# Preparing two units of a decayed linear attention with one scan, in a new written-out order

## The chip, the cores and the metric

The program runs on one core of a Trainium2 chip. The metric is the device time of one execution in microseconds (us). Three runs of the kernel before took 474.7, 475.89 and 476.5 us; the median is 475.89.

## What is computed

Three stages follow each other, in 32-bit arithmetic. The first is a linear attention with a state that decays by channel, for 4 batches, 8 heads, 768 tokens and 48 channels a head:

```
cur   = outer(u * k[t], v[t])
y[t]  = r[t] @ (state + cur)
state = w[t][:, None] * state + outer(k[t], v[t])
```

Its output, 768 x 384 per batch, is the x of a gated block: `h = gelu(x @ w_in)`, its first half u, its second half v normalised over 512 channels; `v_s = w_sg @ v_n + b_sg` mixes the tokens; the result is `x + (u * v_s) @ w_out`. Of that, a third block makes a causal convolution with 5 taps, its sigmoid as a gate, and `(gate * (x @ w_val)) @ w_out2`.

## The kernel before, in words

**Units.** The attention is cut into units: a batch, one of 3 segments of 256 tokens, one of 4 pairs of heads. There are 48, numbered 0 to 47, twelve to a batch. A pair of heads lies on 128 partitions (two times 64, of which 48 carry channels and 16 zeros). Within a unit the tokens are cut into 4 chunks of 64.

**Preparing a unit** (letters are the words of the written-out order). `F` (function `suffix`) is a scan on VectorE over 260 columns that multiplies decays from the right, and a reciprocal of 4 columns; `E` (`prefix`) is a scan from the left which starts each chunk from that reciprocal, in tile D1E. `L` multiplies r by E on GpSimd, `K` multiplies k by F (on GpSimd in batch 0, on VectorE later), and `q` is r times k on VectorE in batches 0 and 1. The input of a unit, decays, k and r, comes in one DMA of 386.5 KB (`pk`); later batches keep two buffers for it.

**Visiting a unit.** TensorE turns k into rows (`t`), makes the 64 x 64 scores of the chunks (`s`), the k-v products (`B`, in `kv`) and the tokens' outputs (`C`). A 32-bit product shows as two matmul records. All of a visit's results share PSUM tile p: k-v products, outputs, transposes and scores have columns of their own in it. The units of odd number in batch 0 use two banks c1 and c2 in its place. Between products ScalarE evicts (`kx`, `gx`, `ox`, `yc`), VectorE masks the scores (`mx`), steps the state (`a`, `z`) and adds outputs (`yx`).

**The dense blocks.** `hv`, `u`, `vs`, `wo`, `val` and `out` are products with 384 or 512 moving columns, three passes each for precision. Words like `vs0` stand for three of them. `ln` normalises a 128 x 512 piece of v: three operations of ScalarE, one of VectorE (`rs`, from the sum of squares), a power on GpSimd, one more of ScalarE and one of VectorE. Weights arrive as 64-bit numbers and are decoded on ScalarE and VectorE (`dec`).

**The order.** The kernel's code writes all instructions into a log under their words; then the string `SCHEDULE` names the words one by one, and each engine gets its instructions in that order. Each engine runs its own list in order and waits at the head of it. Batch 0's attention and the weights' decoding run before the dense products of batch 0; from then on a batch's dense products are interleaved with the visits of the next batch. The last batch has dense products alone. Ahead of the first products, and within and between the visits of batch 0, stand bf16 products on constants, of no use to the result (`wps`, `wm`); three of 256 columns make one word.

The change touches `PARTS` (buffers), `suffix` to `ruk` and `kv` in `unit`, `shared`, `run_loads`, `attention`, `hv`, `out_step`, `first_loads`, and the whole of `SCHEDULE`.

Of the kernel before, what the change touches and what calls it, by code (L numbers as in the profile page):

```python
# [25 lines left out]
C = 64  # L26
# [29 lines left out]
ini0 pk0 zp0 wps0 pk1 pk2 ld0 wl0 ld1 wl1 nat0 F0 wl2 E0 sv0 q0 L0 F1 wl4 K0 pk3 E1 s0 dec0 sv3 wm4  # L56
F2 L1 wl3 wm4 wm0 dec0 t0 K1 q1 nat1 kx0 dec1 t1 dec0 kx1 s1 E2 sv9 B0 dec1 wm1 gx1 L2 mx1 gx2 wm2
mx0 dec1 wm9 dec2 K2 sv10 wm9 dec1 wm10 pk4 gx0 ox0 kx2 B1 dec0 dec4 sv1 wm10 dec2 wm3 a0 dec2 t2 a0
C0 sv2 dec2 sg0 s2 dec1 wm5 ox1 yc0 kx3 wm6 ow2 dec4 gx4 wm7 F3 ow0 sg1 wm8 kx4 gx5 wm11 ow6 K3 z0
wm12 mx2 dec3 wm13 dec0 pk5 gx3 wm15 wl5 ow3 dec4 ox2 pk7 ow7 q2 B2 ow1 dec2 spl1 sv4 wm14 a1 spl0  # L60
dec3 wm15 wm16 a1 dec3 wm16 E3 q3 L3 mx3 yx0 yx1 wm21 dec4 t3 dec3 s3 C1 dec4 wm17 gx7 dec3 wm18
spl10 wm19 F4 yc1 wm20 wl6 ox3 ow5 yd0 wm23 ow9 sv6 spl9 wm21 spl10 K4 wm22 pk6 wm22 spl2 z1 wl7 mx4
E4 yc2 wl8 ow4 U4 sv5 kx5 spl9 L4 gx6 sv7 B3 yx2 pk10 dec5 a2 wm24 sv8 gx8 q4 ow10 s4 sg2 a2 ow8 C2
dec5 F5 pk11 t4 ox5 K5 ox4 mx5 yc3 ow11 z2 ow13 dec5 pk8 wm27 kx6 ow14 E5 wm27 wm28 kx7 U5 wm28 dec5
gx11 pk9 L5 t5 spl3 yx3 gx10 mx6 ow15 dec5 gx9 yd1 wm29 yx4 spl11 a3 s5 q5 ow12 a3 C3 F6 yc4 dec6
nat2 yd2 B4 spl11 K6 wm25 yc5 wm29 yx5 wm30 dec7 mx7 wm30 E6 yd3 ox6 xT0 ow17 wm26 z3 xTo0 spl0 L6
gx12 gx13 xTo0 hv0 kx8 ow19 a4 gx14 spl1 hv0 spl2 t6 dec7 xT1 dec6 a4 s6 dec6 xTo1 B5 dec7 spl5 a4
C4 dec7 spl5 xTo1 hv1 ox7 kx9 U6 mx10 ow18 F7 hv0 spl3 ow20 sg5 gx17 ox8 gx15 ow23 z4 mx8 yc6 kx10
a5 ow16 wm31 K7 ow22 mx9 wm31 yx6 gx16 wm32 q6 ln0 wm32 a5 hv1 dec6 a5 wm33 E7 hv1 F8 spl4 L7 wm33
wm34 ln1 t7 q7 C5 E8 B6 s7 dec7 L8 wm34 gx18 z5 gx20 a6 ow21 K8 kx11 yx7 ln1 gx19 q8 yc7 U7 t8 yd4  # L70
yc8 a6 ox9 s8 spl4 ow26 mx11 B7 spl8 yx8 a6 C6 ow25 sg4 F9 gx23 K9 gx21 z6 U9 wm35 a7 gx22 yd5 ow24
wm35 mx12 wm36 U8 a7 wm36 E9 ow27 ox10 t9 ox11 kx13 kx12 q9 L9 ow31 B8 yx10 ow30 ln0 yx9 ow29 a7 ln0
yc10 s9 F10 ow28 C7 spl8 nat3 sv11 kx14 yc9 ln0 sg3 yx11 xT2 E10 pk12 wm37 ln1 xTo2 wm37 wl9 wm38
gx26 xTo2 hv2 ox12 gx25 K10 gx24 mx13 ln1 z7 a8 wm38 yd6 a8 hv2 ow34 q10 yc11 ow35 a8 yd7 ow33 hv2
F11 U10 L10 ow32 C8 ln2 mx14 B9 ln0 s10 pk13 E11 xT3 t10 q11 wm39 L11 ox14 gx27 wm39 wm40 yc12 gx28
a9 wm40 kx15 K11 yc13 xTo3 yx12 mx15 a9 gx29 s11 q12 kx16 ox13 a9 C9 ow38 ln2 F12 U11 ln2 B10 spl7
K12 ow37 t11 spl7 ow36 wm41 yx13 kx17 xTo3 hv3 gx30 gx32 a10 gx31 yd8 spl6 wm41 wm42 a10 q13 ox15
wm42 ow39 spl6 ow43 mx16 B11 yx14 ln2 mx17 a10 C10 ow40 E12 ow42 yc14 hv3 gx34 F13 L12 ow41 gx33
ox17 hv3 gx35 yx16 ox16 yc15 a11 ow47 yd9 pk14 yx15 yc16 ln1 ow45 s12 ln3 t12 K13 a11 dec6 a11 C11
E13 kx18 wm43 ow44 ln2 L13 ow46 wm43 spl12 nat4 yx17 xT4 mx19 sv12 yc17 F14 yd10 kx19 t13 xTo4 pk15  # L80
s13 spl13 B12 spl12 yd11 ln3 xT5 mx18 dec8 ln3 xTo4 hv4 kx20 spl13 gx36 xTo5 hv4 dec8 ln3 E14 hv4
# [118 lines left out]
def tile_kernel(ctx, tc, pk, sv_, rk_, v_, u_, misc_, w_in, w_sgT, b_sg, w_o1, w_val,  # L200
# [843 lines left out]
```

## Time and profile before

| | |
|---|---|
| median of 3 runs | 475.89 us |
| profiled execution | 474.3 us, span 472.5 us |
| TensorE matmul busy | 450.6 us, 95% of the span |
| weight loads busy | 406.3 us, 86% |
| VectorE busy | 385.0 us, 81% |
| ScalarE busy | 266.9 us, 56% |
| GpSimd busy | 162.3 us, 34% |
| bytes moved | 48.91 MB, mean 103 GB/s |

Times in the profile are us from the start of the span. A busy TensorE is not one at its peak, since the records of pipelined products overlap. PEclk is the share of the full clock that was granted. All instructions carry line 969, the place where the log is played; they are told apart by tile names (vps is `vs`, ups is `u`, c is `wo`, o is `out`, kh and L are `K` and `L`).

### The profile page before, as it was taken

What the parts mean: (1) busy time and instruction counts of PE and PEld (TensorE: products, weight loads), DVE (VectorE), ACT (ScalarE), POOL (GpSimd) and SP (SyncE); (2) the same over time, 40 slices, a digit from 0 to 9 for tenths busy, and PEclk for the clock granted to TensorE, in tenths of its full rate; (3) what the DMA queues carried; (4) which work ended last, traced back from release to release, by engine and by line L of the source; (5) the groups of instructions that cost most, each with busy time, mean ns of one, the idle gap of its engine ahead of it and who ended that gap; (6) DMA issues with size and microseconds to landing.
All of it is one profiled execution on the core that took longest, in us unless ns stands there. A gap on an engine that the chain in (4) does not pass through costs nothing.

```text
span 472.5 us, 13805 instructions
## 1 busy us (share of the span) xinstructions
PE 450.6 (95%) x5556; PEld 406.3 (86%) x5556; DVE 385.0 (81%) x944; ACT 266.9 (56%) x786; POOL 162.3 (34%) x221
## 2 busy tenths in 40 slices
PE   6879899989999999999999999999999999999996
PEld 3666677878979988999999979999999889999995
DVE  5999789999999878978999889847998785337693
ACT  2577789744844469642645388642634696224253
POOL 3245565341622466245132635342213313000200
PEclk9999799999999999999999999999999999999999
DMA  8974053543414452124324522134114000100002
GB/s 278 354 261 167 1 163 111 187 154 114 130 50 116 157 185 68 60 74 152 125 67 135 171 92 85 51 85 135 54 39 147 10 2 1 50 2 0 1 1 100
DMA packets 27088, 48.91 MB, mean 103 GB/s; under 512 B 3088, under 2 KB 17168, under 8 KB 27024
## 3 DMA queue, kind: packets, MB, share of 16 engines
q1 hardware_dynamic: 27024, 48.03, 31.7%
q8 instruction: 43, 0.70, 0.6%
q14 instruction: 21, 0.17, 0.1%
HBM read 43.30 MB, written 4.72 MB: 102 GB/s over the span
## 4 chain that ended last, share of the span: by engine, by line
PE 77%; DVE 9%; ACT 5%; issue 1%; DMA 1%; SPq 0%; ACTq 0%; DVEq 0%
PE vps L969 19%; PE p L969 13%; PE hv L969 10%; PE c L969 9%; PE ups L969 9%; PE o L969 8%; PE val L969 7%; PE a L969 2%; DVE cvp L969 1%; DVE st L969 1%; ACT st L969 1%; ACT vg L969 1%; DVE y L969 1%; DVE F L969 1%; DVE vps L969 1%
## 5 line engine op out<-in xcount | busy, mean ns | idle before, releaser
L969 PE MATMUL vps<-wsg,vnt 128*128 128x384 f32 x576 | 115.5, 339 | 1.4 <-DVE gt L969 0.7
L969 PEld LDWEIGHTS vps<-wsg,vnt 128*128 128x128 f32 x576 | 100.3, 188 | 3.0 <-ACT ut L969 1.6
L969 PE MATMUL ups<-x,win 128*128 128x384 f32 x288 | 61.4, 340 | 0.8 <-DVE gl L969 0.8
L969 ACT ACTIVATE st<-p,F 128x48 f32<-128x48 f32 x144 | 40.3, 304 | 38.0 <-PE p L969 36.7
L969 POOL TENSOR_TENSOR L<-pk,E 128x256 f32<-128x256 f32 x38 | 28.3, 744 | 94.7 <-PE p L969 32.9
L969 PE MATMUL c<-gl,late 128*128 128x384 f32 x288 | 59.9, 339 | 0.0
L969 PE MATMUL hv<-win,x 128*128 128x512 f32 x216 | 59.3, 405 | 0.3 <-ACT x L969 0.3
L969 DVE SCALAR_TENSOR_TENSOR cvp<-x,cw_col,cvp 128x384 f32<-128x384 f32 x84 | 50.6, 613 | 2.1 <-ACT cvp L969 1.6
L969 PEld LDWEIGHTS ups<-x,win 128*128 128x128 f32 x288 | 50.6, 188 | 1.7 <-DVE gl L969 1.1
L969 PEld LDWEIGHTS c<-gl,late 128*128 128x128 f32 x288 | 50.2, 188 | 1.0
L969 DVE SCALAR_TENSOR_TENSOR st<-st,F 128x48 f32<-128x48 f32 x128 | 39.3, 307 | 14.0 <-ACT st L969 13.0
L969 PE MATMUL o<-late,ml 128*128 128x384 f32 x216 | 46.9, 343 | 0.2
L969 PEld LDWEIGHTS hv<-win,x 128*128 128x128 f32 x216 | 38.7, 188 | 8.3 <-DVE x L969 0.9
L969 PE MATMUL val<-x2hl,late 128*128 128x384 f32 x216 | 43.6, 340 | 0.8 <-ACT ut L969 0.8
L969 POOL TENSOR_TENSOR x<-x 128x384 f32<-128x384 f32 x24 | 25.4, 1070 | 44.7 <-DVE cvp L969 43.0
L969 PEld LDWEIGHTS o<-late,ml 128*128 128x128 f32 x216 | 37.9, 188 | 2.8 <-DVE ml L969 1.4
L969 PEld LDWEIGHTS val<-x2hl,late 128*128 128x128 f32 x216 | 37.5, 188 | 1.9 <-ACT ut L969 1.1
L969 ACT ACTIVATE gl<-vps 128x384 fp32r<-128x384 f32 x29 | 14.3, 493 | 33.8 <-DVE vps L969 20.1
L969 POOL TENSOR_TENSOR y<-s,y 128x96 f32<-128x96 f32 x48 | 22.2, 469 | 32.2 <-DVE y L969 17.1
L969 DVE TENSOR_TENSOR_SCAN F<-pk,D1F 128x260 f32<-128x260 f32 x40 | 28.9, 722 | 4.5 <-DMA pk<-in_pk_dram 4.3
L969 POOL TENSOR_TENSOR rstd<-rstd,misc 128x1 f32<-128x1 f32 x24 | 15.6, 650 | 46.0 <-DVE rstd L969 32.3
L969 ACT ACTIVATE ut<-ups 128x384 f32<-128x384 f32 x32 | 15.7, 490 | 25.5 <-PE ups L969 20.6
(133 smaller groups left out, 944.5 us busy)
## 6 DMA issues: line engine op xcount, KB each, us to landing
pk<-in_pk_dram SPq DMA_DIRECT2D x40, 386.5 KB, 3.5
v<-in_v_dram SPq DMA_DIRECT2D x12, 384.0 KB, 4.9
out_dram<-ot SPq DMA_DIRECT2D x24, 192.0 KB, 1.9
rk<-in_rk_dram SPq DMA_DIRECT2D x12, 384.0 KB, 3.3
sv<-in_sv_dram SPq DMA_DIRECT2D x39, 96.0 KB, 3.0
bits<-in_w_in_dram SPq DMA_DIRECT2D x6, 512.0 KB, 7.4
room_l<-in_pk_dram SPq DMA_DIRECT2D x7, 386.5 KB, 6.7
bits<-in_w_o_dram SPq DMA_DIRECT2D x7, 384.0 KB, 4.2
```

The costliest lines, as they stand in the source:

```text
L969: f(*a, **k)
```

## The change

Units are prepared two at a time. Input, F, E, kh and L tiles hold a pair; a pair's decays lie side by side, so one scan of 520 columns, one reciprocal of 8, and one product of 512 do for both. The first two pairs (units 0 to 3) are still prepared unit by unit. Units 4 to 47 make 22 pairs. A pair's input is one DMA of twice the bytes; that of the first pair is four DMAs. In batches 1 to 3 there is one buffer for a pair's input, where there were two for a unit's, one for a pair's kh, and two for a pair's F and L.

```
-    PARTS = {"pk": (PK, 2, "lllllw"), "L": (2 * SEG, 3, "lll"), "sv": (SV, 2, "lllllwwww"),
-             "kh": (SEG, 2, "ww"), "F": (NW + 1, 3, ""), "E": (NW, 1, "w"), "kn": (SEG, 1, "ww"),
-             "D1E": (NW, 1, ""), "st": (SV, 3, ""), "cy": (D, NP, ""), "rk": (2 * DM, 1, "")}
+    PARTS = {"pk": (PK, 1, "lllw"), "L": (4 * SEG, 2, "ll"), "sv": (SV, 2, "lllllwwww"),
+             "kh": (2 * SEG, 1, "ww"), "F": (2 * NW + 1, 2, ""), "E": (2 * NW, 1, "w"), "kn": (SEG, 1, "ww"),
+             "D1E": (2 * NW, 1, ""), "st": (SV, 3, ""), "cy": (D, NP, ""), "rk": (2 * DM, 1, "")}
...
+    def load_pair(n):
+        b, s, p = units[2 * n]
+        t = buf("pk", n, b)
+        cuts = [0, NW + 1, OK_, OR_, PK] if n < 1 else [0, PK]
+        for i, (x, y) in enumerate(zip(cuts, cuts[1:])):
+            with step(f"pku{2 * n}c{i}x"):
+                sp.dma_start(out=t[:, x:y], in_=pk[b, p // 2, s, :, x:y])
...
+    def prep(c, n0, n1):
...
+            if c == "F":
+                dve.tensor_tensor_scan(out=F[:, z:a:-1], data0=w[:, z:a:-1], data1=D1F[:, z:a:-1],
+                                       initial=0.0, op0=ALU.mult, op1=ALU.add)
+                dve.reciprocal(out=d1e[:, a:z:W1], in_=F[:, 1 + a:1 + z:W1])
+            elif c == "E":
+                dve.tensor_tensor_scan(out=E[:, a:z], data0=w[:, a:z], data1=d1e[:, a:z], initial=0.0,
+                                       op0=ALU.mult, op1=ALU.add)
+            elif c == "L":
+                pool.tensor_tensor(out=ch(L[:, t]), in0=ch(r), in1=w1(E[:, a:z])[:, :, 0:C], op=ALU.mult)
+            elif c == "K":
+                (pool if b == 0 else dve).tensor_tensor(out=ch(kh[:, t]), in0=ch(k), in1=w1(F[:, 1 + a:1 + z])[:, :, 1:W1], op=ALU.mult)
+            elif c == "q":
+                dve.tensor_tensor(out=q, in0=r, in1=k, op=ALU.mult)
```

The k-v products of units whose results go to tile p take the 48 columns with channels as weights, not the padded 64. Tile p is allocated once (`ppt`) and written by two constant products at the start; before, each visit allocated it anew. The fillers `wps` move from a bank of the dense products to c0.

```
+                    kwid = D if len(o) == 3 else C
+                    pe.matmul(out=o[c2][64 * hh:64 * hh + kwid, j * D:(j + 1) * D],
+                              lhsT=kn[half[c2], j, hh * C:hh * C + kwid],
...
-                a = psA.tile([128, 2, 512], F32, tag="p", name="p")
+                a = ppt
```

The `rs` of `ln` goes from VectorE to ScalarE, the last eviction is shared between ScalarE and VectorE, and fillers are written after eleven ticks of batch 0, not five: 24 words of three products more.

```
-            dve.tensor_scalar(out=rs, in0=sm[:, 1:2], scalar1=1.0 / DV, scalar2=EPS * DV * DV, op0=ALU.mult, op1=ALU.add)
+            act.activation(out=rs, in_=sm[:, 1:2], func=AF.Identity, scale=1.0 / DV, bias=eps_col)
...
+                    cut = 208 if (b, hf, j) == (B - 1, 1, 2) else DM
+                    act.activation(out=t[:, 0:cut], in_=acc2[0][j][:, 0:cut], func=AF.Copy, scale=0.5)
+                    if cut < DM:
+                        dve.tensor_scalar_mul(out=t[:, cut:DM], in0=acc2[0][j][:, cut:DM], scalar1=0.5)
...
-        if n < 5:
+        if n < 11:
```

The string `SCHEDULE` is written anew. A joined step is `Fu24x0` (pair of units 24 and 25, scan and reciprocal as two words), its load `pku24c0x0`. Shown are its beginning after, the stretch with the first two normalisations before and after, and that with the load for the pair of unit 24 after:

```
+ini0 pku0c1x0 zp1 pku0c0x0 wps0 pku0c2x0 pku0c3x0 ld1 pku2c0x0 Fu1x0 ld0 wl1 Fu0x0 nat0 Fu1x0 Ku1x0
+Eu1x0 wl4 wl0 Ku0x0 sv0 Fu0x0 wl3 Eu0x0 Lu1x0 wm0 qu0x0 wpp0 Lu0x0 wm4 sv1 qu1x0 wl2 s0 Fu3x0 t0 wm4
...
-a5 ow16 wm31 K7 ow22 mx9 wm31 yx6 gx16 wm32 q6 ln0 wm32 a5 hv1 dec6 a5 wm33 E7 hv1 F8 spl4 L7 wm33
-wm34 ln1 t7 q7 C5 E8 B6 s7 dec7 L8 wm34 gx18 z5 gx20 a6 ow21 K8 kx11 yx7 ln1 gx19 q8 yc7 U7 t8 yd4
...
+hv0 dec7 xTo1 spl5 hv1 a4 spl2 ow19 ow18 hv1 ow16 a4 gx14 Eu6x0 ow17 hv1 kx8 a4 C4 ln1 Lu6x0 mx8 z4
+qu6x0 wm34 B5 spl4 s6 t6 hv0 gx15 gx16 zp0 a5 gx17 sg4 hv0 ox8 a5 kx10 dec7 ox7 sg3 yc7 yc6 a5 kx9
+Fu8x0 wm39 wl9 ow21 ln0 wm35 ld3 wm39 wm40*2 dec7 Ku8x0 mx9 B6 yx6 mx10 Fu8x0 C5 Eu8x0 s7 ow23 wm45
...
+qu22x0 U23 s22 U22 sv22 t22 ha0 xTo7 ix3 vs6 pku24c0x0 kx29 ox27 vs6 yc26 gx65 gx64 ix4 wo16 uo7
+outo2 vs6 o20 gx63 vs6 yx26 vs6 a21 yd20 a21 vs6 mx29 wo14 a21 vso6 s23 Fu24x0 C21 B22 t23 gate6 vs7
```

## Rows read from the trace of the kernel before

**Rows 1.** Page, parts 1 and 4: engines' busy time, chain that ended last.

```profile
PE 450.6 (95%) x5556; PEld 406.3 (86%) x5556; DVE 385.0 (81%) x944; ACT 266.9 (56%) x786; POOL 162.3 (34%) x221
...
PE 77%; DVE 9%; ACT 5%; issue 1%; DMA 1%; SPq 0%; ACTq 0%; DVEq 0%
```

**Rows 2.** Windows, each stretch: length, busy us (count) by engine, clock, DMA.

```profile
46.00:52.10 6.10, 4.16 (x98) 2.87 (x96) 4.20 (x13) 5.96 (x18) 2.42 (x3) 1.00 0.05 17
52.10:58.90 6.80, 6.61 (x137) 5.42 (x141) 5.44 (x19) 4.55 (x24) 4.20 (x7) 0.50 0.01 2
60.00:84.00 24.00, 22.22 (x410) 17.18 (x411) 22.68 (x67) 22.88 (x84) 12.90 (x18) 1.00 0.42 131
84.00:108.00 24.00, 21.82 (x274) 19.45 (x276) 22.97 (x67) 12.92 (x38) 8.51 (x11) 1.00 0.54 179
108.00:150.00 42.00, 39.84 (x663) 36.34 (x658) 41.30 (x106) 23.12 (x74) 16.15 (x24) 1.00 0.35 104
150.00:440.00 290.00, 289.94 (x3187) 270.27 (x3179) 227.26 (x531) 158.21 (x434) 94.78 (x129) 1.00 0.26 80
```

**Rows 3.** Windows, VectorE instructions that touch D1E (reciprocals, prefix scans), to 150 us.

```profile
0.00:150.00 150.00, 20.54 (x46) 0.98 0.50 163
```

**Rows 4.** Windows, VectorE instructions that touch rstd, to 150 us.

```profile
0.00:150.00 150.00, 5.26 (x12) 0.98 0.50 163
```

**Rows 5.** Groups of instructions: busy us, mean ns | idle before and its releasers.

```profile
L969 DVE TENSOR_TENSOR_SCAN F<-pk,D1F 128x260 f32<-128x260 f32 x40 | 28.9, 722 | 4.5 <-DMA pk<-in_pk_dram 4.3
...
L969 DVE TENSOR_TENSOR kh<-pk,F 128x256 f32<-128x256 f32 x36 | 17.9, 498 | 0.0
...
L969 DVE RECIPROCAL D1E<-F 128x4 f32<-128x4 f32 x48 | 8.7, 181 | 1.7
...
L969 DVE TENSOR_TENSOR late<-spare,late 128x384 fp32r<-128x384 f32 x10 | 5.6, 556 | 0.0
...
L969 ACT ACTIVATE rsw<-p 128x4 f32<-128x4 f32 (+1 forms) x30 | 5.0, 174 | 3.1 <-PE p L969 3.1
...
L969 DVE TENSOR_TENSOR win<-spare,win 128x512 fp32r<-128x512 f32 x6 | 4.0, 674 | 0.0
...
L969 DVE TENSOR_SCALAR rstd<-sm 128x1 f32<-128x1 f32 x24 | 3.4, 145 | 2.0 <-ACT vnt L969 1.8
```

**Rows 6.** Timeline of VectorE from 46.8 us: start, length, instruction.

```profile
46.82 0.67 DVE L969 TENSOR_TENSOR_SCAN F<-pk,D1F 128x260 f32<-128x260 f32 x1
47.52 0.18 DVE L969 RECIPROCAL D1E<-F 128x4 f32<-128x4 f32 x1
47.61 0.63 DVE L969 TENSOR_TENSOR room_w<-room_w 128x256 f32<-128x256 f32 x1
48.16 0.69 DVE L969 TENSOR_TENSOR_SCAN E<-pk,D1E 128x260 f32<-128x260 f32 x1
```

**Rows 7.** Timeline of TensorE from 68.6 us, one visit of batch 0.

```profile
68.69 0.41 PE L969 MATMUL p<-v,room_w 64*64 64x48 f32 x16
68.92 0.38 PE L969 MATMUL p<-misc,room_l 64*64 64x1 f32 x16
69.23 0.33 PE L969 MATMUL p<-ident,room_w 128*128 128x128 f32 x1
```

**Rows 8.** Timeline of TensorE, a run of fillers.

```profile
17.11 2.47 PE L969 MATMUL wps<-D1F 128*128 128x256 bf16 x21
```

**Rows 9.** The chain in order of time, in the saturated part.

```profile
248.48 1.56 PE vps L969 x9
```

**Rows 10.** DMA issues: count, KB each, median us from issue to landing.

```profile
pk<-in_pk_dram SPq DMA_DIRECT2D x40, 386.5 KB, 3.5
...
room_l<-in_pk_dram SPq DMA_DIRECT2D x7, 386.5 KB, 6.7
```

**Rows 11.** Timeline of VectorE, its first scan.

```profile
4.11 0.70 DVE L969 TENSOR_TENSOR_SCAN F<-pk,D1F 128x260 f32<-128x260 f32 x1 [2.83 <-DMA pk<-in_pk_dram]
```

**Rows 12.** Timeline of ScalarE, the last eviction.

```profile
469.22 0.49 ACT L969 ACTIVATE ot<-o 128x384 f32<-128x384 f32 x1 [0.42 <-DMA out_dram<-ot]
```

More of the change, by code (lines that the diff above doesn't have):

```diff
@@ L71 @@
[L71 to L81, printed above, removed]
@@ new lines @@
+ln0 ow22 t7 ln0 ow20 wm45 wm46 z5 gx18 yx7 ox9 wm46 kx11 a6 Lu8x0 gx19 wm36 gx20 t8 U7 mx11 ln0 B7
+a6 yd4 yx8 s8 ow25 a6 C6 yc8 qu8x0 ow24 yd5 ow27 wm51 ln0 ox11 gx22 wm51 gx21 wm52 gx23 kx13 wm52 a7
+kx12 z6 t9 ow31 a7 yc9 yx10 ox10 ow26 s9 a7 Fu10x0 ln1 C7 ow29 ln1 ow30 B8 ow28 U8 wm37 yx9 U9 yx11
+xT2 spl5 mx12 ox12 gx24 mx13 wm57 z7 xTo2 wm57 wm58 gx25 Ku10x0 xTo2 ow32 sg5 hv2 ow35 mx14 spl7
+Fu10x0 hv2 gx26 Eu10x0 U10 kx14 hv2 yc11 yc10 ow33 a8 wm63 Lu10x0 ln2 a8 wm63 wm58 t10 B9 yd6 a8 s10
@@ L226, in tile_kernel, with cbank @@
     psC = ctx.enter_context(tc.tile_pool(name="psC", bufs=1, space=bass.MemoryType.PSUM))
+    def cbank(i, n, name):
+        return psC.tile([128, n], F32, tag=f"c{i}", name=name)
     ident = const.tile([128, 128], F32, name="ident")
@@ L375, in bonus @@
         s, j = divmod(i, NT)
-        with step("bon"):
+        with step(f"bonb{b}x"):
             t = buf("rk", b * KS + i, b)
@@ L398, in load_sv, with room_q, stages @@
             sp.dma_start(out=buf("sv", n), in_=sv_[b, p, s])
+    def room_q(P, b):
+        return (buf("pk", P, b) if b == 0 else parts["rk"][1][0])[:, 0:2 * SEG]
+    def prep(c, n0, n1):
+        b, s, p = units[n0]
+        P = n0 // 2
+        i0, i1 = n0 % 2, n0 % 2 + n1 - n0
+        a, z = i0 * NW, i1 * NW
+        t = slice(i0 * SEG, i1 * SEG)
+        pkt = buf("pk", P, b)
+        w, k, r = pkt[:, 0:OK_], pkt[:, OK_:OR_][:, t], pkt[:, OR_:PK][:, t]
+        F, E, d1e, kh, L = (buf(x, P, b) for x in ("F", "E", "D1E", "kh", "L"))
+        q = room_q(P, b)[:, t]
+        w1 = lambda x: x.rearrange("p (c t) -> p c t", t=W1)
+        with step(f"{c}u{n0}x"):
+            if c == "F":
[11 more added lines that the diff above has]
+                dve.tensor_tensor(out=q, in0=r, in1=k, op=ALU.mult)
+    def stages(n, which):
+        if n < NU:
+            if n % 2 == 0 and n // 2 < 2:
+                g = (n, n + 1)
+            elif n % 2 == 0:
+                g = (n, n + 2)
+            elif n // 2 < 2:
+                g = (n, n + 1)
+            else:
+                return
+            for c in which:
+                prep(c, *g)
     def unit(n):
         b, s, p = units[n]
-        pkt = buf("pk", n)
-        w, k, r = pkt[:, 0:OK_], pkt[:, OK_:OR_], pkt[:, OR_:OS_]
+        P, i2 = divmod(n, 2)
+        two = slice(i2 * SEG, (i2 + 1) * SEG)
         kn = buf("kn", n).rearrange("p (j t) -> p j t", j=NT)
@@ L409, in unit @@
         first = b == 0
-        kh, F, E, d1e = (buf(x, n) for x in ("kh", "F", "E", "D1E"))
-        L = buf("L", n).rearrange("p (g t) -> p g t", g=2)
+        kh = buf("kh", P, b)[:, two]
+        F = buf("F", P, b)[:, i2 * NW:(i2 + 1) * NW + 1]
+        L = buf("L", P, b).rearrange("p (g i t) -> p g i t", g=2, i=2)[:, :, i2]
         half = [slice(0, 64), slice(64, 128)]
-        e3 = E.rearrange("p (c t) -> p c t", t=W1)
         f3 = F[:, 1:NW + 1].rearrange("p (c t) -> p c t", t=W1)
-        q = pkt[:, 0:SEG] if first else parts["rk"][1][0][:, n % 3 * SEG:(n % 3 + 1) * SEG]
+        q = room_q(P, b)[:, two]
         t = {}
-        def suffix():
-            dve.tensor_tensor_scan(out=F[:, NW:0:-1], data0=w[:, NW:0:-1], data1=D1F[:, NW:0:-1],
-                                   initial=0.0, op0=ALU.mult, op1=ALU.add)
-            dve.reciprocal(out=d1e[:, 0:NW:W1], in_=F[:, 1:NW + 1:W1])
-        def prefix():
-            dve.tensor_tensor_scan(out=E, data0=w[:, 0:NW], data1=d1e, initial=0.0,
-                                   op0=ALU.mult, op1=ALU.add)
-        def r_part():
-            pool.tensor_tensor(out=ch(L[:, 0, :]), in0=ch(r), in1=e3[:, :, 0:C], op=ALU.mult)
-        def k_part():
-            (dve if b > 0 else pool).tensor_tensor(
-                out=ch(kh), in0=ch(k), in1=f3[:, :, 1:W1], op=ALU.mult)
-        def ruk():
-            dve.tensor_tensor(out=q, in0=r, in1=k, op=ALU.mult)
         def turn():
@@ L550, in y_out @@
                 pool.tensor_tensor(out=y, in0=s2[:, ::-1], in1=y, op=ALU.add)
-        steps = {"F": suffix, "E": prefix, "L": r_part, "K": k_part, "q": ruk,
-                "t": turn, "s": scores, "k": k_rows, "m": causal,
+        steps = {"t": turn, "s": scores, "k": k_rows, "m": causal,
                 "B": kv, "o": own_v, "g": grown, "U": carried, "a": states, "z": carry,
@@ L569, in shared @@
             if n < NSEG * NP and n % 2:
-                both[n] = [psC.tile([128, 512], F32, tag=f"c{1 + i}", name=f"p{i}") for i in range(2)]
+                both[n] = [cbank(1 + i, 512, f"p{i}") for i in range(2)]
             else:
-                a = psA.tile([128, 2, 512], F32, tag="p", name="p")
+                a = ppt
                 both[n] = [a[:, 0], a[:, 1], a]
@@ L580, in pair @@
         return [(x.unsqueeze(1), slice(i, i + 1)) for i, x in enumerate(o)]
-    loads = {"pk": load_unit, "sv": load_sv, "rk": load_rk}
+    loads = {"pk": load_pair, "sv": load_sv, "rk": load_rk}
     loaded, user = {"pk": 0, "sv": 0, "rk": 2 * KS}, {}
     def run_loads(kind, done, most=NU):
-        while loaded[kind] < (B * KS if kind == "rk" else NU) and most > 0:
+        while loaded[kind] < {"rk": B * KS, "pk": NU // 2, "sv": NU}[kind] and most > 0:
             n = loaded[kind]
-            t = buf(kind, n, n // KS if kind == "rk" else None)
+            t = buf(kind, n, {"rk": n // KS, "pk": units[2 * n % NU][0], "sv": None}[kind])
             if user.get(id(t), -1) >= done:
@@ L614, in begin @@
                 _, s, p = units[n]
-                go(n, STAGES)
-                if b < 2:
-                    go(n, "q")
-                run_loads("pk", n + 1)
+                stages(n, STAGES)
+                if b >= 2 and n % 2:
+                    run_loads("pk", n // 2 + 1)
                 if p == 0 and b >= 2:
@@ L765, in wo_step @@
         if d == 0:
-            acc[0] = [psC.tile([128, HALF], F32, tag=f"c{f}", name=f"c{f}") for f in range(KD)]
+            acc[0] = [cbank(f, HALF, f"c{f}") for f in range(KD)]
         for f in range(KD):
@@ L778, in wo_step @@
             for f in range(KD):
-                with step("woo"):
+                with step(f"woob{b}h{hf}f{f}x"):
                     xx = x2[:, f, TAPS - 1:]
@@ L828, in out_step @@
         if g == 0:
-            acc2[0] = [psC.tile([128, DM], F32, tag=f"c{f}", name=f"o{f}") for f in range(KD)]
+            acc2[0] = [cbank(f, DM, f"o{f}") for f in range(KD)]
         for j in range(3):
@@ L884, in tile_kernel @@
         dve.memset(D1F, 0.0)
-        dve.memset(D1F[:, 0:NW + 1:W1], 1.0)
+        dve.memset(D1F[:, 0:2 * NW + 1:W1], 1.0)
+    with step("zp"):
+        pool.memset(eps_col, EPS * DV * DV)
     for t in every("D1E"):
@@ L888, in tile_kernel @@
             pool.memset(t, 0.0)
-    wps = psD.tile([128, 512], F32, tag="d", name="wps")
+    wps = cbank(0, 512, "wps")
+    ppt = psA.tile([128, 2, 512], F32, tag="p", name="p")
+    with step("wpp"):
+        for i in range(2):
+            pe.matmul(out=ppt[:, i], lhsT=wsrc[:, 0:128], rhs=wsrc[:, 0:512], start=True, stop=True)
     with step("wps"):
@@ L900, in first_loads @@
         small["U"] = (u_bc, u_.to_broadcast([128, DM]))
-        for c in "kMkvI s sk ks W kskvsk sks BU":
+        for c in "kMkvI s s k s W s vsk s s BU":
             if c in ld:
@@ L986, in pack @@
     kr[..., 0:D, 1, :] = tr(r)
-    flat = lambda a: a.reshape(lead + (128, -1))
-    return np.concatenate([flat(dec), np.zeros(lead + (128, 1), f), flat(kr)], axis=-1)
+    two = lambda a, g: a.reshape(B, NP // 2, 2, NSEG, 128, g, -1).transpose(0, 1, 3, 4, 5, 2, 6).reshape(
+        B, NP // 2, NSEG, 128, -1)
+    return np.concatenate([two(dec, 1), np.zeros((B, NP // 2, NSEG, 128, 1), f), two(kr, 2)], axis=-1)
 def pack_v(v):
```

299 lines of the change are left out of this document (156 added, 143 removed).

## The prediction

> **What bounds the kernel now.** I read the page first: TensorE is busy 95% of the span, and 77% of the chain that ended last lies on it [rows 1]. That is an average over two very different parts, so the windows come next [rows 2]. From 150 to 440 us TensorE has 289.94 of 290 us busy and VectorE 227.26: there only fewer or shorter products help, and 62.7 us of VectorE are spare. From 60 to 150 us it is the other way round. VectorE has 22.68 of 24, 22.97 of 24 and 41.30 of 42 us; TensorE has 6.1 us idle in the three windows together, and what it does there includes fillers. Two short windows stand out in between. [...] So the order of limits is: VectorE to about 150 us, with one ScalarE stall and one slow-clock stretch inside it, then TensorE to the end.
>
> **Joined preparation.** What counts is the instructions that vanish before 150 us. 46 VectorE instructions touch D1E by then [rows 3], which are 23 reciprocals and 23 prefix scans: units 0 to 22 are prepared, and unit 23 is next. Units 4 to 23 become 10 pairs. Each loses a scan F, a reciprocal, a scan E and a product q: 40 instructions; the 6 pairs of batch 1 also lose a K on VectorE: 6. rstd is touched 12 times by 150 us [rows 4], that is 6 normalisations, whose 6 `rs` go to ScalarE. Together 52.
>
> An instruction that vanishes saves its fixed part alone, for its columns stay. Two products on the same engine, 384 columns in 556 ns and 512 in 674 ns, give 0.92 ns a column and some 200 ns at no columns; the reciprocal of 4 columns takes 181 ns [rows 5]. That is the upper bound: 52 x 0.18 = 9.4 us. But records overlap: the reciprocal begins at 47.52 and the next product at 47.61 [rows 6], so the engine is held 0.09 us: lower bound 52 x 0.09 = 4.7 us. I take 0.09 for the ten reciprocals, 0.18 for the ten F scans (the reciprocal begins only after the scan's end at 47.49) and 0.12 for the other 32, nearer to the row that shows the next start: 0.9 + 1.8 + 3.8 = **6.5 us** off VectorE before 150 us. [...]
>
> Not all of the 6.5 can arrive. TensorE has only 6.1 us idle from 60 to 150 us [rows 2], and both engines full at once is not to be had while each waits for the other. I charge **+2.0** (between 0, were all idle time waits for VectorE, and 4, were two thirds of the gain stopped by products). After 150 us the savings of the other 12 pairs and 18 normalisations lie under TensorE and count nothing; without that cover they would be 12 x 5 x 0.12 us, about 7.
>
> **The `rs` on ScalarE.** The nearest row is rsw, a tiny eviction of 174 ns [rows 5], against 145 ns on VectorE. Six before 150 us add 1.0 us to ScalarE, which has 22.88 of 24 us from 60 to 84 [rows 2]. Bounds 0 and 1.0; I take **+0.3**, since only a third of that stretch is so tight. [...]
>
> **The new order at 46 to 59 us.** Before, ScalarE's parts of the two first normalisations follow each other with one other ScalarE word (`spl4`) between; the evictions of the visits wait behind, TensorE starves, and the clock falls. After, `ln1` and `ln0` have ten ScalarE words between them (spl4, gx15 to gx17, ox7, ox8, kx9, kx10, yc6, yc7). VectorE's holes there are 1.9 us (6.10 - 4.20) and 1.36 us (6.80 - 5.44) [rows 2]: bounds 0 and 3.3. I take half, **-1.6**, because the clock may fall again at another place.
>
> **More fillers.** 24 words of three products; 21 took 2.47 us [rows 8], so 0.118 each and 72 x 0.118 = 8.5 us. They stand in TensorE's queue: where it waits anyway they are free, else what is behind them, transposes and scores for which ScalarE and VectorE wait, is late. Counting in the written-out order, some 7 extra words stand before `xT2` (59 us before), some 6 between there and `u0` (84 us), and ten between `u1` and `vs3` (85 to 102 us). The last ten cost 3.5 us where TensorE is idle 2.2 us of 24 [rows 2]. Bounds 0 and 8.5; I take **+1.5**, the excess of those ten with a little.
>
> **48 weights in place of 64.** In one visit 16 k-v records with 48 moving columns start at 68.69, the next 16 records with one moving column at 68.92, and the transposes at 69.23 [rows 7]. So 16 records take 0.23 us, and with one column instead of 48 still 0.31 with the change to a full transpose. The moving columns don't set the pace; the weights or the issue do. If the issue, nothing is gained; if the weights, a quarter: 0.0575 us a unit. 26 units (22 to 47) fall in the saturated part: 0 to 1.5 us; I take **-1.2**, since the pace hardly rises with one moving column, and both have 64 columns of weights. [...]
>
> **A pair's load.** It may be issued only when F, E, L, K and q of the pair before are through with the one buffer; the joined F is in VectorE's queue, with masks, state steps and gates behind it, for which TensorE waits. Three 384-column products take 0.52 us [rows 9]; counting those between the load's word and its scan, for unit 24 seven and one set of scores, gives 4.0 us of cover. For the pairs of 12 to 22 the same count gives 4.0, 5.4, 6.5, 5.5, 5.7 and 5.3 us; after that 4.0 to 18. A load of 386.5 KB lands in 3.5 us, and in 6.7 in the crowded start [rows 10]. Twice the bytes: between 3.5 and 7.0 us; I take 4.7. Then only unit 12's is late, **+0.7**, and what is late after 150 us falls into VectorE's spare time.
>
> **Start, tail, tile p.** The first scan waits 2.83 us for 386.5 KB [rows 11]; its load is now a third of that, but three more transfers are issued before the first unit is complete, and GpSimd makes both units' K first. Bounds -1.0 and +0.9 (one L or K late); I take -0.4. The last eviction of 0.49 us [rows 12] is shared: 0 to -0.25, I take -0.15. One allocation of tile p in place of 42 lets a visit's products wait for the columns they write, not for all readers of the visit before; in the saturated part nothing waits, so 0, with up to -1 before.
>
> **Sum.** -6.5 + 2.0 + 0.3 - 1.6 + 1.5 - 1.2 + 0.7 - 0.4 - 0.15 = -5.35 us. Against the profiled execution's 474.3 us (span 472.5, 1.8 around it) that is 468.95. The median shown, 475.89, is 1.6 above that execution, so I expect **470.5 us** in such runs. Faster, same and slower mean by more or less than 0.5%, which is about what a measurement of this kernel can tell from no change: below 473.5, to 478.3, above.
>
> **Rivals.**
> (a) More arrives: the stall and the slow clock go whole (3.3 for 1.6), nothing is charged for products in the way (2.0), the fillers find only holes (1.5). 470.5 - 1.7 - 3.5 = 465.3. For it: 60 to 150 us has 6.1 us of TensorE idle and fillers besides. Against: two full engines rarely mesh.
> (b) The clock falls again, in a new place, and holes as before open: +1.6 and a little behind it, 472.5. For it: one drop came in a stretch that had fillers; against: there are more of them.
> (c) The preparation is not what VectorE is short of; ScalarE or the chain between visits takes its place as soon as it is shorter. Then weights, start and tail remain: 475.89 - 1.75 = 474.1. For it: ScalarE's 22.88 of 24; against: its load falls to 12.92 of 24 in the next window while VectorE's stays.
> (d) Slower: the pair's load is too late. It decides when a landing takes longer than the cover, about 5.3 us. At 7.0 us the pairs of 12 to 22 are late by 3.0, 1.6, 0.5, 1.5, 1.3 and 1.7, 9.6 us on VectorE's queue while it is the limit; 8.9 more than I charge: 479.4. For it: 6.7 us for half the bytes early on. Against: 3.5 us is the median, and the transfers share the queue with little else then.
> That the change doesn't do what it says has no room here, since fewer instructions are issued whatever the time.
>
> **How the numbers follow.** Forecast 0.47, (a) 0.15, (b) 0.12, (c) 0.13, (d) or another loss of the new order 0.13. Faster: the forecast, (a) and nine tenths of (b), with (c) on the border giving little: 0.72. Same: 0.15. Slower: 0.13. The likeliest case alone runs from 467.5 to 473; the range that leaves two in ten out reaches to (a) and past (c), 464 to 477.
>
> **What would show it.** Right: 827 VectorE instructions in place of 944; VectorE's sum before the first product `vs6` (156 us before) smaller by 6 to 7 us, and that product 3 to 5 us earlier; no window with a clock of 0.50 behind the start; 16 k-v records in 0.17 to 0.18 us; the saturated part with no idle time. Wrong: waits of F on a pk load above 1 us in batch 1; `vs6` no earlier; TensorE holes at new places after 150 us.

## The result, and the profile after

The changed kernel took 471.1 us (median of 4 runs, 470.36 to 471.92); the kernel before took 475.58 beside it. The ratio is 0.9901, with a 95% interval of 0.9873 to 0.9929. Two more sets of runs gave 0.9905 (0.9884 to 0.9925) and, on another chip, 0.9933 (0.9913 to 0.9952). So it is faster by 0.7 to 1.0%, 3.1 to 4.5 us. The profiled execution took 470.36 us, with a span of 468.5. The log is now played at line 1028.

The page after, parts 1, 2 (the granted clock) and 4, answers to [rows 1]:

```profile
PE 453.8 (97%) x5630; PEld 410.5 (88%) x5630; DVE 373.0 (80%) x827; ACT 269.8 (58%) x810; POOL 156.4 (33%) x196
...
PEclk9889999999999999999999999999999999999999
...
PE 83%; DVE 3%; ACT 1%; POOL 1%; issue 1%; DMA 0%; ACTq 0%; POOLq 0%
```

VectorE lost 117 instructions and 12 us of busy time, and its share of the chain fell from 9% to 3%. TensorE's share rose from 77% to 83%: the kernel is limited by products over more of its span.

The windows of [rows 2], after (columns as there):

```profile
46.00:52.10 6.10, 6.10 (x117) 5.00 (x116) 4.61 (x13) 6.00 (x27) 2.94 (x4) 1.00 0.39 134
52.10:58.90 6.80, 6.03 (x186) 4.85 (x185) 6.41 (x20) 5.59 (x26) 4.75 (x6) 1.00 0.01 2
60.00:84.00 24.00, 21.95 (x417) 17.17 (x417) 23.22 (x51) 21.34 (x78) 9.87 (x14) 1.00 0.30 98
84.00:108.00 24.00, 23.73 (x328) 21.16 (x328) 23.93 (x60) 14.08 (x43) 9.32 (x10) 1.00 0.53 179
108.00:150.00 42.00, 42.00 (x639) 39.97 (x632) 40.44 (x94) 23.91 (x79) 14.55 (x20) 1.00 0.38 121
150.00:440.00 290.00, 289.96 (x3202) 270.80 (x3201) 216.61 (x467) 160.02 (x451) 94.43 (x120) 1.00 0.24 78
```

The slow stretch at 52.1 us is gone, but VectorE is as full as before from 60 to 150 us, with fewer instructions in the same windows. The slow clock has moved to two other places, 3.4 us each, as two windows after show:

```profile
12.60:16.00 3.40, 3.40 (x57) 2.47 (x57) 2.37 (x4) 0.61 (x3) 1.96 (x3) 0.50 1.03 403
26.30:29.70 3.40, 3.40 (x18) 2.30 (x17) 3.40 (x9) 3.00 (x12) 1.93 (x2) 0.50 0.93 282
```

To place the gain I set the dense products of the two traces side by side, the first with the first and so on: how much earlier does the changed kernel start the same number of them? At 53 us (by the kernel before) it is level, at 63 (behind the old slow stretch) 2.6 us earlier, at 79 within 0.6, from 97 to 106 it is 2.4 to 3.7 us *later*, at 120 level, from 138 to 150 it is 2.2 to 4.5 us earlier, and at the end 4.4. So nothing is left of what the first 100 us won, where the new order, the fillers and the split start were to pay.

### The profile page after: what moved, and what is told of

Same layout as the page of the kernel before. It is cut to its first block, busy times and chain, and to the rows that moved or that the text cites. A ratio compares the mean times of both kernels' runs of the same rounds, so it can differ in the third digit from the quotient of the medians.

```text
span 468.5 us, 13743 instructions
## 1 busy us (share of the span) xinstructions
PE 453.8 (97%) x5630; PEld 410.5 (88%) x5630; DVE 373.0 (80%) x827; ACT 269.8 (58%) x810; POOL 156.4 (33%) x196
## 4 chain that ended last, share of the span: by engine, by line
PE 83%; DVE 3%; ACT 1%; POOL 1%; issue 1%; DMA 0%; ACTq 0%; POOLq 0%
PE vps L1028 21%; PE p L1028 13%; PE c L1028 11%; PE ups L1028 10%; PE hv L1028 9%; PE val L1028 8%; PE o L1028 8%; PE a L1028 1%; PE wps L1028 1%; DVE spare L1028 1%; DVE vnt L1028 1%; DVE st L1028 0%; DMA out_dram<-ot 0%; ACT vg L1028 0%; POOL wsg L1028 0%
## 5 line engine op out<-in xcount | busy, mean ns | idle before, releaser
L1028 PE MATMUL ups<-x,win 128*128 128x384 f32 x288 | 59.9, 339 | 0.0
L1028 ACT ACTIVATE st<-p,F 128x48 f32<-128x48 f32 x144 | 38.7, 305 | 35.6 <-PE p L1028 35.4
L1028 PE MATMUL hv<-win,x 128*128 128x512 f32 x216 | 57.8, 404 | 0.2 <-DVE x L1028 0.2
L1028 POOL TENSOR_TENSOR L<-pk,E 128x512 f32<-128x512 f32 (+1 forms) x20 | 23.1, 1158 | 70.9 <-DVE E L1028 35.1
L1028 POOL TENSOR_TENSOR x<-x 128x384 f32<-128x384 f32 x24 | 24.2, 1016 | 44.6 <-DVE cvp L1028 39.2
L1028 PEld LDWEIGHTS <-D1F 128*128 128x128 bf16 x270 | 25.8, 104 | 11.7 <-issue 5.0
L1028 POOL TENSOR_TENSOR rstd<-rstd,misc 128x1 f32<-128x1 f32 x24 | 17.0, 707 | 46.2 <-ACT rstd L1028 34.9
```

Source lines behind the costliest of these rows:

```text
L1028: f(*a, **k)
```

## The experiments

Twelve kernels, with 5 to 12 runs each. The first four ran on one chip, the other eight on a second one, where the changed kernel stood at 0.9933 and not at 0.9905. Each ratio is to the kernel before on the same chip; differences are taken between medians, to the changed kernel on that chip, unless the text says otherwise. Over all 186 runs of this study, each against its own kernel's mean, 0.01 of mean granted clock goes with 2.4 us; where the text says what goes with the clock, it is an estimate by that slope.

**e1_after_again**: no edit. 

> The changed kernel as it is, beside the three variants of it on the same chip. Expected 471.1 us, as measured before, within 0.7 us.

Measured: 469.86 us, 0.9905 (0.9884 to 0.9925). The first result repeats.

**e2_single**: the joined steps of units 4 to 47 are issued as two single ones in the same places of the order.

```
-    prep(c, *g)
+    for part in (0, 1) if c == "F" else (None,):
+        for m in range(*g):
+            prep(c, m, m + 1, g[0], part)
```

> The changed kernel with every joined step of units 4 to 47 issued as two steps of one unit each, at the same places of the order; buffers, loads, weights, fillers and order stay. 94 instructions come back on VectorE, 46 of them before 150 us. Theory (VectorE is the limit up to 150 us, and what the joined steps save there arrives in part): 46 x 0.125 us = 5.8 us more on VectorE, of which 3 to 4.5 arrive: 474.5 us. Rival (the new order made the gain, and VectorE had slack in it): 471.1 plus at most 0.7 us.

Measured: 475.73 us, 1.0032 (1.0018 to 1.0045), 5.9 above e1_after_again; 0.6 of it goes with the clock (mean 0.993 in its runs, 0.996 in the five of e1_after_again). The joining is worth more than the whole gain: without it the kernel is slower than before. VectorE's sum up to the same dense product, in e2_single and then after:

```profile
0.00:160.30 160.30, 147.37 (x382) 0.98 0.48 161
```

```profile
0.00:155.30 155.30, 141.38 (x335) 0.98 0.50 167
```

With 47 instructions fewer VectorE is held 6.0 us less, and the product comes 5.0 us earlier: most of it arrives. The dense products of both kernels stand in the same order; side by side, the changed kernel's are 1.8 us ahead at 41 us, 5.0 at 152 and 5.4 at the end.

**e3_nofill**: the 24 added words of fillers are left out. 

> The changed kernel without the 24 added words of fillers (three constant products each, ticks 5 to 10 of batch 0). Theory (the fillers that stand between the first dense products, 85 to 104 us, are in the way): the products after them start earlier by 2 to 3 us and half of that stays at the end, 469.5 us. Rival (they hold the clock or fill holes only): the clock falls to 0.50 for some 6.8 us between 40 and 105 us and the time is 472.5 to 474 us; or, with holes only, 471.1 us.

Measured: 472.31 us, 0.9956 (0.9937 to 0.9975), 2.4 above e1_after_again. The rival held: the fillers pay. Its windows at the slow clock:

```profile
12.00:18.80 6.80, 6.07 (x69) 4.43 (x70) 4.09 (x9) 3.35 (x11) 1.86 (x2) 0.50 1.04 409
39.30:42.70 3.40, 2.80 (x13) 2.40 (x14) 3.10 (x9) 2.41 (x7) 2.91 (x4) 0.50 0.45 148
100.80:104.20 3.40, 3.40 (x77) 3.31 (x67) 3.40 (x7) 1.16 (x5) 1.72 (x2) 0.50 0.70 220
```

That is 13.6 us at 0.50 where the changed kernel's profile has 6.8. The first of the three stretches lies ahead of all words left out, which begin at 33 us; the other two lie among them. Its mean clock over 12 runs is 0.986, that of the five runs of e1_after_again beside it 0.996; 2.3 us of the 2.4 go with that.

**e4_w64**: `kwid = C`, 64 columns of weights again. 

> The changed kernel with 64 columns of weights in all k-v products, as before. Theory (the weights set the pace): 16 records take 0.25 us in place of 0.21 and the 26 units of the saturated part cost 1.0 us more, 472.1 us. Rival (the issue sets it, or the work behind absorbs it): no difference above 0.3 us.

Measured: 472.76 us, 0.9968 (0.9942 to 0.9994), 2.9 above e1_after_again; 0.6 goes with the clock (0.993 against 0.996). Its runs spread from 469.9 to 476.6. Set beside the profile after, product by product, its trace loses 2.7 us between 104 us and the end. 1.3 of them come bit by bit behind 131 us, with the visits (below). The other 1.4 come between 120 and 131 us, where TensorE once waits 1.2 us for VectorE (`cy`). The windows, in e4_w64 and then after:

```profile
121.00:124.00 3.00, 1.81 (x11) 1.51 (x10) 2.97 (x6) 2.15 (x6) 1.55 (x2) 1.00 0.39 119
```

```profile
121.00:124.00 3.00, 3.00 (x33) 2.75 (x35) 3.00 (x8) 2.31 (x6) 1.51 (x2) 1.00 0.71 211
```

Whether that wait belongs to the edit one trace doesn't show.

**e5_order**: all edits of instructions undone (single steps, 64 weights, `rs` on VectorE, no added fillers); the new order, its buffers, the pairs' loads, tile p's one allocation and the shared last eviction remain. 

> The changed kernel's order, buffers and pair loads with the old instructions: single steps for units 4 to 47, 64 weights, rs on VectorE, no added fillers. Theory (the parts found so far add up: joined steps 5.9 us, fillers 2.3, weights 1 to 2, rs some 0.4, and the order itself gives nothing without them): 470 + 5.9 + 2.3 + 1.5 + 0.4 = 480 us, 1.2% slower than the kernel before. Rival (the order itself is better and the parts overlap): the time of the kernel before, 474 us, or less.

Measured: 479.5 us, 1.0098 (1.0062 to 1.0134), 5.3 above the kernel before. The new order by itself loses; 2.0 us of the 5.3 go with the clock (mean 0.984 against 0.992).

**e6_rsdve**: `rs` on VectorE again. 

> The changed kernel with rs of the normalisation on VectorE again. Theory (VectorE is the limit to 150 us): six short instructions more there, 6 x 0.065 to 0.15 us, so 0.4 to 0.9 us slower, 470.5 us where the changed kernel takes 469.9. Rival (ScalarE is as tight there): 0 to 1 us faster.

Measured: 471.3 us, 0.993 (0.9908 to 0.9952), the same as e9_after below (0.9933). The move is worth nothing that shows.

**e7_nolate**: only the last 11 of the 24 added filler words are left out. 

> The changed kernel without eleven of the added words of fillers, wm48 to wm50, wm53 to wm56, wm59, wm60 to wm62: those that stand behind u1, beside the first dense products. Theory (fillers there are no cover for the clock, since dense products keep TensorE busy, and they delay): the clock stays at full speed and the time falls by 0.5 to 1.5 us, 468.9 us. Rival (they hold the clock there): the clock drops to 0.50 at about 101 us as in the run without any, and the time is 470 to 471.5 us.

Measured: 472.26 us, 0.9955 (0.9933 to 0.9976), 0.7 above e9_after (1.0 by the ratios) with overlapping intervals; both the theory's 468.9 and the rival's range are missed. The 3.5 us that they were to cost between 85 and 102 us don't come back: set beside e9_after, product by product, its trace is 0.8 us behind at 85 us, where the words left out begin, and 1.0 at 169.

**e8_beforefill**: 24 filler words put into the kernel before, between the steps of visits 5 to 10. 

> The kernel before with the 24 words of fillers added, two behind each of the k-v products and token products of ticks 5 to 10 (42 to 70 us), all else as before. Theory (the slow clock at 52 to 59 us goes and its wait with it): 1 to 2.5 us faster than the kernel before. Rival (TensorE only waits for ScalarE and VectorE there, so a faster clock is worth nothing and the fillers delay): 0 to 3 us slower.

Measured: 479.66 us, 1.0107 (1.0076 to 1.0139), 5.5 slower. Its windows of [rows 2]:

```profile
52.10:58.90 6.80, 5.94 (x131) 4.69 (x128) 4.45 (x15) 5.27 (x26) 2.61 (x5) 1.00 0.02 5
60.00:84.00 24.00, 22.72 (x467) 17.28 (x466) 20.26 (x61) 20.02 (x76) 14.19 (x19) 1.00 0.41 122
```

The clock is full (mean 0.999 over the runs), yet VectorE has 3.7 us of holes from 60 to 84 us, where it had 1.3. From 52 to 84 us VectorE waits 4.9 us for ScalarE's evictions `st`, where it waited 1.3, which fits fillers that stand in TensorE's queue ahead of the products that ScalarE evicts. So a full clock alone did not make that kernel faster. One difference is left untested: these fillers write to a bank of the dense products, as those of the kernel before do, where the changed kernel's write to c0.

**e9_after**: no edit, beside the last three. 

> The changed kernel once more, to be compared with the three kernels beside it. Both theories: 469.9 us, 0.990 of the kernel before (0.988 to 0.993).

Measured: 471.57 us, 0.9933 (0.9913 to 0.9952), a little more than expected.

**e10_orderfill**: as e5_order, with the added fillers kept. 

> The new order with its loads of a pair, its buffers and its 24 added filler words, but with single preparation steps, 64 weights and rs on VectorE. Without the fillers this kernel took 479.5 us, with some 15 us at a granted clock of 0.50. Theory: the fillers are worth the 2.4 us that leaving them out of the changed kernel cost, and the rest of the loss lies in the order itself: 477 us (475.5 to 478.5), 1.003 to 1.009 of the kernel before. Rival 1: the loss of the order is all clock, which the fillers give back: 475 us or less, at or below the kernel before. Rival 2: the fillers only pay where the joined steps leave room beside them, as in the kernel before, where they cost 4 us or more: 479.5 us or more.

Measured: 478.13 us, 1.0071 (1.0042 to 1.0099), 3.5 above the kernel before and 6.6 above e9_after. The theory held: the fillers give 1.4 back, the order keeps its loss. Two of the runs had a mean clock of 0.996, against 0.992 over the runs of the kernel before, and still took 476.8 and 477.0 us. So the clock isn't the reason of that loss.

**e11_split2**: the second pair's input in four pieces too, decays ahead of the constants.

```
-    cuts = [0, NW + 1, OK_, OR_, PK] if n < 1 else [0, PK]
+    cuts = [0, NW + 1, OK_, OR_, PK] if n < 2 else [0, PK]
```

> The load of the second pair comes in four pieces too, its decays ahead of the small constants. In the trace of the changed kernel VectorE waits 2.4 us for that load at 8 to 10 us. Theory: the wait shrinks to under 1 us, the clock and the queue of loads stay as they are, and what the start gains is carried to the end: 468.9 us (468.3 to 469.5), 1 us less than the changed kernel beside it. Rival: the first units are paced by what comes after this scan (the weights' and constants' landings, now three transfers later), so the wait only moves: 469.9 to 470.9 us.

Measured: 471.98 us, 0.9937 (0.9915 to 0.9959). The rival held: VectorE no longer waits for the second pair (its scan starts at 7.69 us), and nothing arrives at the end.

**e12_one**: the first pair's input in one DMA, `cuts = [0, PK]` for all. 

> The first pair's input comes in one DMA, as all the others do. Theory: the first scan waits for 772.5 KB instead of the decays' third of it, some 1.5 to 2 us longer, and the start carries that to the end: 471.4 us (470.6 to 472.2). Rival, by the term of the prediction (the split start is worth 0.4 us at most, since VectorE has room before the first visits): 469.9 to 470.3 us.

Measured: 468.96 us, 0.9882 (0.9852 to 0.9911), 2.6 below e9_after: the fastest version, against the theory's 471.4 and also below the rival's 469.9. VectorE's first rows, in e12_one and then in e9_after:

```profile
5.12 1.29 DVE L1028 TENSOR_TENSOR_SCAN F<-pk,D1F 128x260 f32<-128x260 f32 x2 [3.57 <-DMA pk<-in_pk_dram]
...
9.96 1.28 DVE L1028 TENSOR_TENSOR_SCAN F<-room_l,D1F 128x260 f32<-128x260 f32 x2
```

```profile
3.04 1.29 DVE L1028 TENSOR_TENSOR_SCAN F<-pk,D1F 128x260 f32<-128x260 f32 x2 [1.49 <-DMA pk<-in_pk_dram]
...
9.12 1.29 DVE L1028 TENSOR_TENSOR_SCAN F<-room_l,D1F 128x260 f32<-128x260 f32 x2 [1.39 <-DMA room_l<-in_pk_dram]
```

The first scan is 2.1 us later, the second pair's only 0.8. Its mean clock over the runs was 0.995 against 0.992, which goes with 0.6 us. The two profiled executions differ by 0.7 us only (469.49 and 470.23). What makes up the other 2 us of the medians is not settled.

## Why the prediction was right in its sum and wrong in its steps

470.5 us was forecast and 471.1 measured, but the terms of the sum missed by several us in both directions.

**Joined preparation: the sum came out partly by luck, and the charge of +2.0 was too much.** The groups of the changed kernel that answer to [rows 5]:

```profile
L1028 DVE TENSOR_TENSOR_SCAN F<-pk,D1F 128x520 f32<-128x520 f32 x19 | 23.7, 1245 | 0.6 <-DMA pk<-in_pk_dram 0.5
L1028 DVE TENSOR_TENSOR kh<-pk,F 128x512 f32<-128x512 f32 x18 | 12.5, 697 | 1.3 <-PE p L1028 1.2
L1028 ACT ACTIVATE rstd<-sm,eps_col 128x1 f32<-128x1 f32 x24 | 7.1, 296 | 0.0
L1028 DVE RECIPROCAL D1E<-F 128x8 f32<-128x8 f32 x22 | 4.4, 198 | 0.0
```

By these means and those of [rows 5] one joined scan takes 1245 ns where two took 2 x 722, 199 saved, and a joined K saves 2 x 498 - 697 = 299. But the means hold single long records (see the new order below). By the medians up to the first `vs6`, in e2_single and after, a scan takes 1235 ns for 2 x 688, a product 679 for 2 x 415 and a reciprocal 199 for 2 x 160: 141, 151 and 121 saved.

The forecast of 6.5 us off VectorE stands beside 6.0 in the trace (e2_single). To see what they consist of I cut every VectorE record that exceeds the median of its form (operation, columns, type) in its run by more than 0.15 us back to that median, and summed again. The 47 instructions are then worth 2.9 us (138.2 and 135.3), 0.06 each, since records overlap: less than the 0.09 that I had taken for the lower bound. The other 3.1 us are long records that the joined form avoids (9.1 us of lengthening became 6.1), a gain that the prediction did not have. Net of the charge 4.5 were to arrive; 5.0 do up to that product, and 5.9 between the medians.

**The new order: the step that failed.** It was put at -1.6, with +0.7 for the pair's load and -0.4 for the start: -1.3 together. e5_order has these, with the shared eviction (-0.15) and tile p's one allocation (0), and is 5.3 us *slower* than before; e10_orderfill, whose mean clock is that of the kernel before (0.991), 3.5. I counted only the ScalarE stall and the slow clock at 46 to 59 us, and took the rest of the order as neutral for VectorE, the engine that sets the pace there. The slow clock left that place; ScalarE is still full (6.00 of 6.10 us from 46 to 52.1), but TensorE's holes beside it have gone. The pair's load is not to blame: in the whole changed kernel F waits 1.9 us for `pk`, 1.4 of it at the first scan, and 2.4 us for the second pair (tile room_l), in e10_orderfill 1.9 and 1.0; the pair lands in 4.5 us where 4.7 was taken:

```profile
pk<-in_pk_dram SPq DMA_DIRECT2D x19, 772.5 KB, 4.5
```

The traces show where the loss sits. The state step on VectorE, same shape and count up to the same dense product, in the kernel before, in e10_orderfill, and after:

```profile
L969 DVE SCALAR_TENSOR_TENSOR st<-st,F 128x48 f32<-128x48 f32 x36 | 9.8, 271 | 3.5 <-ACT st L969 3.2
```

```profile
L1038 DVE SCALAR_TENSOR_TENSOR st<-st,F 128x48 f32<-128x48 f32 x36 | 13.3, 370 | 2.8 <-ACT st L1038 2.3
```

```profile
L1028 DVE SCALAR_TENSOR_TENSOR st<-st,F 128x48 f32<-128x48 f32 x36 | 12.4, 346 | 2.2 <-ACT st L1028 1.7
```

The mean grows from 271 to 370 ns because single ones of them take 0.4 to 1.1 us. One such place after, on VectorE and then on GpSimd:

```profile
52.73 0.87 DVE L1028 SCALAR_TENSOR_TENSOR st<-st,F 128x48 f32<-128x48 f32 x1
53.52 0.35 DVE L1028 TENSOR_TENSOR y<-p,y 128x192 f32<-128x192 f32 x1
53.79 0.26 DVE L1028 SCALAR_TENSOR_TENSOR st<-st,F 128x48 f32<-128x48 f32 x1
```

```profile
52.35 1.18 POOL L1028 TENSOR_TENSOR L<-room_w,E 128x512 f32<-128x512 f32 x1
```

The step lasts until GpSimd's product ends (53.5 to 53.6 us); 1 us later the same instruction takes 0.26. Running beside a product is not enough. In the kernel before, on VectorE and then on GpSimd:

```profile
81.82 0.26 DVE L969 SCALAR_TENSOR_TENSOR st<-st,F 128x48 f32<-128x48 f32 x1
```

```profile
81.32 0.69 POOL L969 TENSOR_TENSOR L<-pk,E 128x256 f32<-128x256 f32 x1 [1.45 <-issue]
```

Here the step begins 0.19 us before the product's end. Up to the first `vs6`, 18 state steps of the kernel before run beside a GpSimd product of 256 or more columns, and 4 of them take over 0.4 us; the others begin in its last 0.25 us or ahead of it. In e10_orderfill it is 13, of which 12 take over 0.4 us: they begin 0.37 to 1.0 us before its end, and all 12 end 0.06 to 0.07 us behind it. Why a step ends with the product, the traces do not show.

By the count of long records above, over all VectorE instructions up to the first `vs6`, lengthening holds VectorE 3.7 us before, 9.6 in e5_order, 9.8 in e10_orderfill, 9.1 in e2_single and 6.1 after. A GpSimd instruction runs beside every one of the records cut (13 before, 31 in e10_orderfill), but only beside about half of all VectorE instructions. VectorE's sum up to that product in e10_orderfill, to be set beside the line of the kernel before further down:

```profile
0.00:161.30 161.30, 148.02 (x385) 0.95 0.47 157
```

It is 4.8 us above that of the kernel before with 4 instructions fewer, `vs6` comes 4.9 us later, and VectorE's idle time is the same (13.3 and 13.2 us). So the loss up to there lies in longer records and not in waits. (This execution is the slowest of its kernel, 480.93 us.)

So the new order starts VectorE's state steps and other instructions early in GpSimd's products, not near their ends: 6.1 us more by this count, while the time grew by 3.5 to 5.3. That is read from traces; no run here moved GpSimd's products away, so it is not shown by experiment. Nor did any kernel join the steps in the old order: e5_order and e10_orderfill put two single steps where the new order has a joined one, so their loss is that of this order with single steps.

**The fillers: wrong sign.** +1.5 was forecast; they are worth -2.4 in the changed kernel (e3_nofill) and -1.4 without the joined steps (e5_order to e10_orderfill). I counted them as time in TensorE's queue alone. With them the mean clock is higher, 0.996 against 0.986 and 0.991 against 0.984, which goes with 2.3 and 1.8 us, as much as they are worth; and the ten that were to cost most show no cost (e7_nolate). That they can cost as much as was feared shows in the kernel before (+5.5, e8_beforefill).

**48 weights: the term held.** One visit in e4_w64 (64 columns) and then after (48), the 16 k-v records and the record after them:

```profile
237.58 0.45 PE L1028 MATMUL p<-v,kn 64*64 64x48 f32 x16
237.85 0.30 PE L1028 MATMUL p<-st,L 64*64 64x48 f32 x8
```

```profile
236.75 0.40 PE L1028 MATMUL p<-v,kn 64*48 64x48 f32 x16
236.97 0.30 PE L1028 MATMUL p<-st,L 64*64 64x48 f32 x8
```

From start to next start 0.27 us becomes 0.22. The visits of the two kernels stand in the same order: of the 23 sets behind 131 us whose 16 records are all in both traces, 20 differ by 0.052 to 0.054 us and three by 0.04; over the 27 visits seen behind 150 us that makes 1.2 us, the -1.2 taken. So 0.0575 was nearly right as a difference. The size of a set was not: [rows 7] showed a short one, and 16 records take 0.215 us in most visits, not 0.17 to 0.18.

**`rs` on ScalarE: +0.3 against nothing.** The instruction takes 296 ns, not the 174 taken from its nearest row. It costs no time that shows (471.3 us without it in e6_rsdve, 471.57 with it in e9_after); ScalarE has 21.34 of 24 us from 60 to 84 where it had 22.88.

**Start and tail.** The first scan begins at 2.97 us, 1.1 earlier than in [rows 11], as the split promised. But the second pair's scans begin at 9.90 us where the third unit's began at 8.33, since they wait 2.4 us for a pair's load, and e12_one, without the split, is faster. Nor does an earlier second pair help (e11_split2). What the first 10 us of VectorE are worth to the end stays open. The last eviction takes 0.34 us on ScalarE where it took 0.49, the -0.15 taken; no run tests it.

**The sum.** On the second chip the order with its fillers cost 3.5 us (e10_orderfill against the kernel before) and the joined steps with the weights gave 6.6 (from e10_orderfill to e9_after). The prediction had +0.05 (-1.6 + 0.7 - 0.4 + 1.5 - 0.15) and -5.4. That 470.5 came so near to 471.1 is luck: the order's neutral rest on one side, and the charges on joining and fillers and the long records that joining avoids on the other, worked against each other.

**What was to show it.** Right: 827 instructions; `vs6` at 152.37 us, 4.0 earlier; the saturated part without idle time; no wait of F above 1 us in batch 1. Wrong: VectorE's sum before `vs6`, which fell by 2.6 and not by 6 to 7. In the kernel before and then after:

```profile
0.00:156.40 156.40, 143.22 (x389) 0.98 0.49 160
```

```profile
0.00:152.40 152.40, 140.58 (x333) 0.98 0.49 166
```

56 instructions fewer and 2.6 us less means that others became longer: by the count of long records the fewer instructions take 5.0 us off, and lengthening adds 2.4 (3.7 to 6.1). Wrong too: the k-v records (0.215 us) and the slow clock, which moved.

## What to carry to other kernels

Joining two small scans or products shortens their records by 0.12 to 0.15 us here, but frees the engine by only some 0.06, since records overlap; look for what else the joined form avoids. A new order is not neutral because its instructions are the same: count for each long GpSimd product which VectorE steps begin early in it (12 of the 13 state steps beside one took over 0.4 us in e10_orderfill, 4 of 18 in the kernel before). Set two kernels whose products stand in the same order side by side, product by product: that places an effect which the medians blur. Test an order with the other edits undone before its gain is credited to any of them, and fillers in the order in which they will run.

## What was not expected of the hardware

The granted clock of one and the same kernel differs from run to run: the changed kernel had 0.50 at 12.6 to 16.0 and at 26.3 to 29.7 us in one profile, and in another (e1_after_again) at one place near the start:

```profile
13.50:16.90 3.40, 3.40 (x19) 2.35 (x17) 2.19 (x6) 3.19 (x10) 0.93 (x1) 0.50 1.06 417
```

With its mean clock between 0.986 and 0.996 its 21 runs went from 468.9 to 473.5 us, the slowest three at 0.986 to 0.989. An effect under 1 us needs more than one profile of each side here.
